# Two of four weight products in float16 pairs instead of float32r pairs, in a windowed-attention, SoLU-MoE and rational-MoE kernel

## The chip, the cores and the metric

The kernel runs on one core of a Trainium2 chip. The metric is the time of one execution on the device in microseconds, lower is better; before the change the median of three runs is 745.09 us (744.92 to 745.19).

## The reference

Attention with a causal window of 128 keys and a linear bias per head (4 batches, 8 heads, 576 positions, 64 wide) gives 2304 tokens of 512 numbers. Two feed-forward blocks follow. All is wanted in about float32 precision.

```python
scores = scale * q @ k.T + bias ; masked to 0 <= rel < 128 ; softmax ; @ v     # 2304 x 512
# first MoE, d_ff = 1024
h = x @ w_in
solu = h * softmax(h)
ln = (solu - mu) / np.sqrt(var + 1e-06) * g_ln
x = ln @ w_out
# second MoE, d_ff = 2048
h = x @ w_in
P = a[0] + a[1] * h + a[2] * h2 + a[3] * h3
Q = 1.0 + np.abs(b[0]) * np.abs(h) + np.abs(b[1]) * h2
out = (P / (Q + 1e-06)) @ w_out
```

## The kernel before, in words

Weights and inputs come as float64 where the reference gives them so; `decode` (lines 489 to 503) turns a raw piece of 128 x 512 into float32 with one ScalarE and two VectorE operations. Each of the four weight products then works on **pairs**: an operand is split into an upper part and the rest, both float32r, and three products (upper x upper, rest x upper, upper x rest) are summed in PSUM. So each product costs three TensorE passes.

The work runs in tiles of 128 tokens (18 of them). `scores` and `attend` do the attention of a tile, from tile 5 on in 16-bit parts whose transposes go by DMA (line 700). `moe_in` (780) is the first product of the first MoE: 24 matmuls of 512 columns a tile, at line 788. `moe_tr` (835) transposes its result into `lh`, `ll` at lines 845 and 846. `moe_out` (850) does two tiles at a time, 96 matmuls of 256 columns at line 863, with stationary `woh`, `wol` (w_out times the gains g_ln, split by `split_w`, 533), copies the sums into `ys` and stores them to `yT` in DRAM. The second MoE runs over groups of 512 tokens (four, and one of 256) and 16 steps `f` of 128 hidden units. `ff_in` (933) makes h in one PSUM bank with 12 matmuls at line 942, then eleven elementwise operations (lines 962 to 980) on ScalarE and VectorE, and the split into `gh`, `gl` (helpers `copy`, line 468 to 470, and `less`, line 479 and 480). `ff_out` (986) takes these as stationary operands of 12 matmuls of 512 columns at line 1003. Its weights come through `early_w2` (887), which decodes 28 pieces during the first stage and parks them in DRAM, and `split_w2` (901), which reloads and splits them; `load_y` (917) reloads and splits the tokens.

The order of all this is not written by hand. Each operation is put on a list with an engine (or several possible), a modelled duration and a due time `pri`; `Plan.order` (158) lays them out by a list schedule when the program is built, and the engines then execute that fixed order. The table `PR` holds the due times and offsets by stage and engine, `SLOTS` the number of buffers of each kind. Where TensorE would have nothing in the first 50 us of the plan, a filler matmul on zeros is put there (line 1073, bfloat16, 256 columns). SBUF has two regions a side: `left1` and `right1` for the first stage, `left2` and `right2` for the second MoE; a later region opens when the earlier one is wholly free.

Of the kernel before, what the change touches and what calls it, by code (L numbers as in the profile page):

```python
# [7 lines left out]
F32 = mybir.dt.float32  # L8
F32R = mybir.dt.float32r
# [14 lines left out]
    "bias": -3.593, "biash": -2.341, "load": 3.531, "load0": 5.238, "hold": 2, "merge": 8, "loadv0": 4.2,  # L24
    "loadv": 4.079, "v": 1.842, "s": 1.742, "pv": 0.742, "win": -1.048, "wout": 0.37, "wstep": 0.368,
    "tr": -0.218, "mo": 2.066, "e0": 3.565, "e1": 12.092, "npre": 28, "plain": 5, "ln": 'dve',
    "alt.dve": 1500.0, "alt.act": 393.9, "alt.pool": -274.9, "ahead": 5.989, "warm": 50000.0,
    "cold": 6800.0, "pein": 1, "peout": 0, "last": 0.16, "scores.dve": -0.358, "scores.pool": 0.961,
    "scores.pe": -0.3, "moe_in.dve": 0.79, "attend.act": -0.139, "moe_out.pool": 0.119,
    "scores.act": 0.342, "moe_in.act": 2.074, "attend.dve": 0.102, "moe_tr.pe": -0.442,  # L30
    "moe_out.dve": -0.69, "moe_out.act": 0.25, "split_v.dve": -0.139, "moe_out.pe": 0.224,
    "weights.dve": 0.16, "weights.act": -0.169, "weights.pool": -0.155,
# [289 lines left out]
def t_pe(n, cols, wide=True):  # L322

    return n * (cols * 0.4167 + ((17.0 if cols > 256 else 13.3) if wide else 4.0))
# [20 lines left out]
def kernel(  # L345
# [119 lines left out]
    def copy(out, i, n, r, w, pri, psum=False, first="act", on=("act", "dve", "pool")):  # L465

        alts = {
            "act": (t_act(n, psum), lambda: nc.scalar.activation(out=out(), in_=i(), func=ACTF.Copy), False),  # L468
            "dve": (t_dve(n, not psum), lambda: nc.vector.tensor_copy(out(), i()), not psum),
            "pool": (t_pool(n, False), lambda: nc.gpsimd.tensor_scalar(  # L470
                out(), i(), 1.0, 0.0, ALU.mult, ALU.add), True),
        }
# [59 lines left out]

# [582 lines left out]
```

## Time and profile before

| | |
|---|---|
| median of 3 runs | 745.09 us |
| span of the profiled execution | 744.7 us |
| TensorE busy / VectorE / ScalarE / GpSimd | 736.3 / 585.1 / 479.3 / 318.8 us |
| TensorE weight loads busy | 631.6 us |
| matmuls of line 863 / 942 / 1003 / 788 | 864 / 960 / 864 / 432 |

The median lies 0.4 us above the profiled span. In the profile PE is TensorE's matmuls, PEld its weight loads, DVE VectorE, ACT ScalarE, POOL GpSimd, SP the queue that issues DMAs. A matmul's recorded duration (371 ns on average at line 942) is its passage through a pipeline; the pace of a run of matmuls is read from the start-to-start distance, that is from the length of a run in the chain divided by its count.

### The profile page before, as it was taken

The page shows a single profiled execution, that of the slowest core. Times are in us where ns is not written, and L with a number is a line of the kernel's source. Part 1 is how long each engine was busy: PE and PEld are TensorE (multiplying, and loading weights), DVE is VectorE, ACT ScalarE, POOL GpSimd, SP SyncE. Part 2 cuts the span into 40 slices and gives each one's busy share as a digit, 9 for nine tenths or more (in the row PEclk, how much of TensorE's full clock was granted, in tenths as well). Part 3 has the DMA queues.
Part 4 walks back from the last instruction along what each step waited for, and adds up shares of the span by engine and source line. Part 5 has one row for each costly group of instructions (what it writes and reads, how often), then busy time and mean ns, then how long its engine had stood idle before and what let it go on. Part 6 is the DMA issues. An engine that isn't in the chain of part 4 may idle for free.

```text
span 744.7 us, 14059 instructions
## 1 busy us (share of the span) xinstructions
PE 736.3 (99%) x5184; PEld 631.6 (85%) x5184; DVE 585.1 (79%) x1259; ACT 479.3 (64%) x950; POOL 318.8 (43%) x319
## 2 busy tenths in 40 slices
PE   8999999999999999999999999999999999999997
PEld 7889989898898999899788888888888888888896
DVE  4999788887888754456989897779977788877984
ACT  6887665755656555365997776557755666566783
POOL 1524444445544734065895633334233443332421
PEclk9999999999999999999999999999999999999999
DMA  8933899999999835063651210000100001000010
GB/s 317 302 132 81 191 266 256 249 279 206 263 233 200 163 79 93 17 212 106 191 155 57 73 62 1 0 1 22 57 1 1 0 1 58 0 1 0 1 58 29
DMA packets 107349, 82.19 MB, mean 110 GB/s; under 512 B 57616, under 2 KB 89360, under 8 KB 107280
## 3 DMA queue, kind: packets, MB, share of 16 engines
q1 hardware_dynamic: 107280, 81.29, 41.3%
q8 instruction: 41, 0.67, 0.4%
q14 instruction: 28, 0.23, 0.1%
HBM read 51.39 MB, written 16.78 MB: 92 GB/s over the span
## 4 chain that ended last, share of the span: by engine, by line
PE 95%; DVE 2%; ACT 1%; DMA 1%; SPq 0%; issue 0%; POOL 0%; POOLq 0%; DVEq 0%
PE bk L942 26%; PE bk L1003 14%; PE h L788 14%; PE bk L863 13%; PE h L1003 11%; PE bk L639 4%; PE bk L768 4%; PE bk L616 3%; PE bk L743 2%; PE bk L1073 2%; PE bk L685 1%; DMA dx<-w2i 1%; DVE bk L965 0%; ACT s L669 0%; DVE bk L976 0%; DVE tcc L980 0%
## 5 line engine op out<-in xcount | busy, mean ns | idle before, releaser
L942 PE MATMUL bk<-yh,wb 128*128 128x512 f32 (+1 forms) x540 | 133.3, 371 | 0.2 <-DVE tcc L974 0.2
L480 POOL TENSOR_TENSOR gl<-tcc,gh 128x512 fp32r<-128x512 f32 x63 | 82.0, 1301 | 85.5 <-PE bk L1003 54.9
L942 PEld LDWEIGHTS bk<-yh,wb 128*128 128x128 f32 x540 | 97.2, 188 | 21.4 <-DVE tcc L974 0.4
L962 ACT ACTIVATE bk<-bk,bcoef 128x512 f32<-128x512 f32 (+1 forms) x80 | 49.6, 620 | 91.7 <-PE bk L942 91.6
L942 PE MATMUL bk<-yh,wa 128*128 128x512 f32 (+1 forms) x420 | 101.9, 371 | 1.1 <-DVE tcc L974 0.9
L942 PEld LDWEIGHTS bk<-yh,wa 128*128 128x128 f32 x420 | 75.0, 188 | 17.5 <-DVE tcc L974 1.7
L965 DVE SCALAR_TENSOR_TENSOR bk<-tb,nb,bk 128x512 f32<-128x512 f32 (+1 forms) x80 | 56.0, 700 | 42.7 <-ACT tb L964 42.6
L1003 PE MATMUL bk<-wo,gh 128*128 128x512 f32 x288 | 88.5, 394 | 0.0
L863 PE MATMUL bk<-lh,woh 128*128 128x256 f32 x288 | 84.1, 292 | 0.0
L863 PE MATMUL bk<-ll,woh 128*128 128x256 f32 x288 | 81.5, 283 | 0.0
L863 PE MATMUL bk<-lh,wol 128*128 128x256 f32 x288 | 81.4, 283 | 0.0
L669 ACT ACTIVATE s<-s,nm 128x256 f32<-128x256 f32 (+1 forms) x144 | 63.6, 489 | 19.9 <-DVE nm L662 19.7
L1003 PE MATMUL h<-wo,gh 128*128 128x512 f32 x240 | 74.9, 393 | 0.9 <-POOL gh L470 0.9
L470 POOL TENSOR_SCALAR gh<-tcc 128x512 fp32r<-128x512 f32 (+1 forms) x42 | 26.1, 622 | 94.9 <-DVE tcc L980 75.9
L480 POOL TENSOR_TENSOR pl<-s,ph 128x512 f16<-128x512 f32 (+1 forms) x51 | 61.4, 1215 | 9.0 <-ACT ph L468 6.2
L1003 PEld LDWEIGHTS bk<-wo,gh 128*128 128x128 f32 x288 | 53.4, 188 | 11.3
L976 DVE SCALAR_TENSOR_TENSOR bk<-bk,qc,tb 128x512 f32<-128x512 f32 (+1 forms) x80 | 56.3, 704 | 7.2 <-ACT tb L969 5.3
L662 DVE CUSTOM_DVE_ANT_0 s<-bk,bias 128x256 f32<-128x256 f32 (+1 forms) x144 | 50.9, 404 | 11.9 <-PE bk L639 10.4
L970 ACT ACTIVATE tcc<-bk,acoef 128x512 f32<-128x512 f32 (+1 forms) x80 | 59.3, 741 | 0.2 <-POOL gh L480 0.2
L967 ACT ACTIVATE tb<-bk,qc 128x512 f32<-128x512 f32 (+1 forms) x80 | 51.9, 648 | 11.3 <-DVE bk L965 10.9
L974 DVE SCALAR_TENSOR_TENSOR tcc<-tcc,acoef,bk 128x512 f32<-128x512 f32 (+1 forms) x80 | 55.5, 693 | 2.3
L980 DVE SCALAR_TENSOR_TENSOR tcc<-tcc,acoef,bk 128x512 f32<-128x512 f32 (+1 forms) x80 | 55.4, 693 | 2.2
(174 smaller groups left out, 1816.8 us busy)
## 6 DMA issues: line engine op xcount, KB each, us to landing
rw<-in_moe_w_in_dram SPq DMA_DIRECT2D x18, 512.0 KB, 4.9
rw<-in_moe_w_out_dram SPq DMA_DIRECT2D x16, 512.0 KB, 4.6
kn<-in_k_dram SPq DMA_DIRECT2D x18, 256.0 KB, 5.1
qn<-in_q_dram SPq DMA_DIRECT2D x18, 256.0 KB, 3.9
vv<-in_v_dram SPq DMA_DIRECT2D x18, 256.0 KB, 4.4
yT<-ys SPq DMA_DIRECT2D x18, 256.0 KB, 3.2
yr<-yT SPq DMA_DIRECT2D x16, 256.0 KB, 3.4
w2i<-dc SPq DMA_DIRECT2D x15, 256.0 KB, 3.4
```

The source lines that it names most:

```text
L480: "pool": (t_pool(n), lambda: nc.gpsimd.tensor_tensor(out(), a(), b(), op), True),
L669: nc.scalar.activation(out=s[:, jj, 0:W], in_=s[:, jj, 0:W], func=ACTF.Exp, scale=-1.0, bias=nm[:, h:h + 1], accum_out=sm[:, h:h + 1] if p ...
L788: nc.tensor.matmul(h[:, cols], a[:, kk], w[:, kk, cols], start=(i == 0 and kk == 0), stop=(i == 2 and kk == KD - 1))
L863: nc.tensor.matmul(y[:, r], w[:, f, cols], x[:, f % 4], start=(f == 0 and n == 0), stop=(f == KF - 1 and n == 2))
L942: nc.tensor.matmul(h(), w[:, a, kk], y[:, b, kk, 0:n], start=(i == 0 and kk == 0), stop=(i == 2 and kk == KD - 1))
L965: o("dve", t_dve(n) + 60, lambda: stt(out=A(), in0=R(), scalar=nb1, in1=A(), op0=ALU.mult, op1=ALU.subtract), [bR], [bA])
L967: o("act", t_act(n, True, ptrs=1), lambda: act(out=R(), in_=A(), func=ACTF.Ln, scale=-1.0, bias=qc), [bA], [bR])
L970: o("act", t_act(n, True, 2), lambda: act(out=C(), in_=h(), func=ACTF.Identity, scale=acoef[:, 3:4], bias=acoef[:, 2:3]), [hb, "coef"], [bC])
L974: o("dve", t_dve(n) + 60, lambda: stt(out=C(), in0=C(), scalar=acoef[:, 1:2], in1=h(), op0=ALU.add, op1=ALU.mult), [hb], [bC])
L976: o("dve", t_dve(n) + 60, lambda: stt(out=A(), in0=A(), scalar=qc, in1=R(), op0=ALU.subtract, op1=ALU.mult), [bR], [bA])
L980: o("dve", t_dve(n) + 60, lambda: stt(out=C(), in0=C(), scalar=acoef[:, 0:1], in1=A(), op0=ALU.add, op1=ALU.mult), [bA], [bC])
L1003: nc.tensor.matmul(acc[g][s][2](), a(slice(s * P, (s + 1) * P)), w[:, c], start=(f == 0 and i == 0), stop=(f == KF2 - 1 and i == 2))
```

## The change

`moe_out` and `ff_in` get float16 pairs where they had float32r pairs; `moe_in` and `ff_out` stay float32r. Since float16 has a narrow range, the weights are scaled by powers of two found on the chip. `squares` sums the squares of each of the 8 pieces of w_out (times g_ln) and of the 16 pieces of the second w_in on ScalarE. `scale_to_range` takes the largest sum, spreads it over the partitions by one TensorE product with ones, and makes a power of two and its inverse with some ten tiny VectorE operations. `scaled_gains` then splits all 8 pieces of w_out, which wait decoded in a float32 buffer `wof`; `split_w2` splits each piece of w_in by ScalarE or GpSimd and VectorE. The powers are taken back in factors that were there before (`hc` in place of the coefficients), in the copy to `ys` and in the copy of the outputs. The normalised tokens carry a factor 2^10.

The numbers of buffers and the due times are dealt anew, and the early pieces of the second MoE's w_in come sooner than those of w_out (16 and 12 of the 28, before 15 and 13).

```diff
 PR = {
-    "bias": -3.593, ... "loadv": 4.079, "v": 1.842, "s": 1.742, "pv": 0.742, "win": -1.048, "wout": 0.37, "wstep": 0.368,
-    "tr": -0.218, "mo": 2.066, "e0": 3.565, "e1": 12.092, "npre": 28, "plain": 5, "ln": 'dve',
-    ... "ahead": 5.989, ...
+    "bias": -1.592, ... "loadv0": 5.697, "loadv": 5.377, "v": 1.039, "s": 1.964, "pv": 0.916, "win": -1.733,
+    "wout": 0.079, "wstep": 0.041, "tr": -5.062, "mo": 2.534, "e0": 3.645, "e1": 12.42, "npre": 28,
+    ... "ahead": 1.425, ... "weights.dve": 2.246, "weights.act": -2.496, "weights.pool": -0.392,
 SLOTS
-        "e": 1, "u": 2, "lh": 2, "ll": 3, "rw": 2, "ys": 3, "dc": 3, "st": 6,
+        "e": 1, "u": 2, "lh": 2, "ll": 3, "rw": 2, "ys": 4, "dc": 3, "st": 5,
-        "qn": 2, "kn": 5, "vv": 3, "v2": 4, "s": 5, "ph": 1, "pl": 2, "pth": 3, "ptl": 3,
-        "xr": 3, "xh": 3, "xl": 4, "nm": 3, "sm": 3,
+        "qn": 2, "kn": 5, "vv": 3, "v2": 2, "s": 5, "ph": 1, "pl": 3, "pth": 3, "ptl": 2, "xr": 5,
+        "xh": 5, "xl": 6, "nm": 6, "sm": 3, "tn": 1,
-        "wa": 7, "woa": 1, "gh": 3, "gl": 2, "yh0": 1, "yr": 5, "wr": 1, "dx": 3, "tb": 2,
-        "tcc": 3,
+        "wa": 7, "woa": 1, "gh": 4, "gl": 2, "yh0": 1, "yr": 4, "wr": 4, "dx": 4, "tb": 3, "tcc": 8,
-        "wb": 9, "wo": 15, "yh1": 1, "ob": 3,
+        "wb": 9, "wo": 15, "yh1": 1, "ob": 2,
...
-    woh = w1.tile([P, KF, DM], F32R, name="woh")
-    wol = w1.tile([P, KF, DM], F32R, name="wol")
+    wof = w1.tile([P, KF, DM], F32, name="wof")
+    woh = w1.tile([P, KF, DM], F16, name="woh")
+    wol = w1.tile([P, KF, DM], F16, name="wol")
...
+    def squares(x, xa, at, key, pri, by=None):
+        plan.op("act", t_act(512, ptrs=1 if by is None else 2), lambda: nc.scalar.activation(
+            out=junk, in_=xa(), func=ACTF.Square, scale=1.0 if by is None else by(), accum_out=sums[:, at:at + 1]),
+            r=[x] + ([] if by is None else ["gsb"]), w=[key], pri=pri)
+
+    def scale_to_range(name, lo, hi, keys, pri):
...
+        tiny(lambda: V.tensor_reduce(out=top(), in_=sums[:, lo:hi], axis=AX.X, op=ALU.max), keys)
+        plan.op("dve", 200, lambda: V.tensor_scalar(d.t, ident, top(), None, ALU.mult), r=[m], w=[d], pri=pri)
+        plan.op("pe", 235.0, lambda: nc.tensor.matmul(b.t, ones, d.t, start=True, stop=True), r=[d], w=[b], pri=pri)
...
+    def scaled_gains(pri):
+        scale_to_range("o", 0, KF, [("sums", f) for f in range(KF)], pri)
...
+        for f in range(KF):
...
+            split_scaled(x, lambda f=f: wof[:, f], lambda f=f: woh[:, f], lambda f=f: wol[:, f],
+                         ("woh", f), ("wol", f), gain, "gs", pri)
...
-            part = (lambda: woh[:, f], lambda: wol[:, f], ("woh", f), ("wol", f))
-            gain = lambda: gsb[:, f:f + 1]
...
-                split_scaled(x, *part, gain, pri)
+            squares(x, xa, f, ("sums", f), pri, by=lambda: gsb[:, f:f + 1])
...
-            lT[pr] = [(Buf("lh", [P, 4, 2 * P], F32R), Buf("ll", [P, 4, 2 * P], F32R)) for _ in range(2)]
+            lT[pr] = [(Buf("lh", [P, 4, 2 * P], F16), Buf("ll", [P, 4, 2 * P], F16)) for _ in range(2)]
...
-            copy(lambda ys=ys: ys.t, lambda y=y: y.t, 512, [y], [ys], pri, psum=True)
+            copy(lambda ys=ys: ys.t, lambda y=y: y.t, 512, [y], [ys], pri, psum=True, by=2.0 ** -20)
...
+        if kind == "i":
+            squares(x, lambda: flat(x.t), KF + f, ("sums", KF + f), pri)
...
-        w = Buf(group, [P, 2] + shape2[kind], F32R)
+        w = Buf(group, [P, 2] + shape2[kind], F16 if kind == "i" else F32R)
...
-        split(x, lambda: x.t, lambda: w[:, 0], lambda: w[:, 1], (w, 0), (w, 1), 512, pri)
+        if kind == "i":
+            split_scaled(x, lambda: x.t, lambda: w[:, 0], lambda: w[:, 1], (w, 0), (w, 1),
+                         lambda: power["i"][:, 0:1], ("power", "i"), pri)
+        else:
+            split(x, lambda: x.t, lambda: w[:, 0], lambda: w[:, 1], (w, 0), (w, 1), 512, pri)
...
-        y = Buf(f"yh{g % 2}", [P, 2, KD, 512], F32R)
+        y = Buf(f"yh{g % 2}", [P, 2, KD, 512], F16)
...
-        o("act", t_act(n, True, 1), lambda: act(out=A(), in_=h(), func=ACTF.Abs, scale=bcoef[:, 0:1]),
-          [hb, "coef"], [bA])
+        o("act", t_act(n, True, 1), lambda: act(out=A(), in_=h(), func=ACTF.Abs, scale=hc[:, 4:5]),
+          [hb, "hc"], [bA])
...
         copy(lambda ob=ob: ob.t, src[2], 512, [src[1]], [ob], pri - 4.0, psum=True,
-                     first="act" if s % 2 != last else "dve")
+                     first="act" if s % 2 != last else "dve", by=lambda: hc[:, 2:3])
...
-    pieces = sorted([(f - 2.0, "i", f) for f in range(KF2)] + [(f, "o", f) for f in range(KF2)])
+    pieces = sorted([(f - 4.0, "i", f) for f in range(KF2)] + [(f, "o", f) for f in range(KF2)])
...
+    scaled_coefs(PR["e0"] + PR["e1"] + 0.3)
```

## Rows read from the trace of the kernel before

**Rows 1.** The page: busy time of each engine, and TensorE's granted clock in 40 slices.
```profile
PE 736.3 (99%) x5184; PEld 631.6 (85%) x5184; DVE 585.1 (79%) x1259; ACT 479.3 (64%) x950; POOL 318.8 (43%) x319
...
PEclk9999999999999999999999999999999999999999
```

**Rows 2.** Waits of engine PE: us in total, times, longest us.
```profile
PE bk L1073 <- DVE still L440: 1.8, 1, 1.8
PE bk L942 <- DVE tcc L974: 1.0, 3, 0.7
PE h L1003 <- POOL gh L470: 0.9, 1, 0.9
```

**Rows 3.** Stretches: length; PE, PEld, DVE, ACT, POOL busy us; PEclk; DMA share; GB/s.
```profile
20.00:50.00 30.00, 30.00 (x277) 26.54 (x276) 28.05 (x78) 26.61 (x73) 14.16 (x13) 1.00 0.75 252
50.00:100.00 50.00, 50.00 (x378) 44.76 (x378) 43.14 (x126) 35.67 (x80) 19.01 (x18) 1.00 0.59 146
...
150.00:200.00 50.00, 50.00 (x534) 45.19 (x531) 39.75 (x122) 30.43 (x64) 23.68 (x25) 1.00 1.03 245
...
300.00:350.00 50.00, 49.72 (x389) 45.06 (x388) 26.36 (x50) 24.20 (x46) 19.84 (x17) 1.00 0.35 111
350.00:400.00 50.00, 49.31 (x214) 39.70 (x213) 44.74 (x61) 43.00 (x74) 41.91 (x37) 1.00 0.49 153
400.00:420.00 20.00, 20.00 (x88) 16.17 (x87) 18.74 (x30) 13.13 (x21) 12.57 (x13) 1.00 0.15 53
420.00:440.00 20.00, 20.00 (x89) 16.39 (x88) 18.48 (x25) 16.27 (x28) 9.96 (x9) 1.00 0.24 75
...
550.00:600.00 50.00, 50.00 (x217) 40.46 (x217) 39.46 (x55) 29.15 (x49) 19.26 (x21) 1.00 0.00 0
```

**Rows 4.** Chain that ended last, in time: start us, us, what, matmuls in a row.
```profile
17.31 1.09 PE bk L1073 x10
...
36.47 1.73 PE bk L743 x16
...
114.03 1.24 PE bk L768 x40
...
332.82 11.51 PE bk L863 x96
```

**Rows 5.** Groups, shapes apart: count, busy us, mean ns, idle before: splits and sums.
```profile
L480 POOL TENSOR_TENSOR wb<-dx,wb 128x512 fp32r<-128x512 f32 x8 | 10.4, 1298 | 2.8 <-ACT wb L468 2.8
L480 POOL TENSOR_TENSOR wa<-dx,wa 128x512 fp32r<-128x512 f32 x7 | 9.8, 1416 | 0.9 <-ACT wa L468 0.7
L479 DVE TENSOR_TENSOR wo<-dx,wo 128x512 fp32r<-128x512 f32 x3 | 5.3, 1754 | 0.5 <-POOL wo L470 0.5
L519 DVE SCALAR_TENSOR_TENSOR wol<-dc,gsb,woh 128x512 fp32r<-128x512 f32 x6 | 5.0, 832 | 0.5 <-POOL woh L513 0.5
L815 ACT ACTIVATION_READ_ACCUMULATOR e<-u,st 128x1 f32 x18 | 3.4, 187 | 0.0
L511 ACT ACTIVATE woh<-dc,gsb 128x512 fp32r<-128x512 f32 x2 | 1.4, 716 | 0.9 <-DVE dc L501 0.9
```

**Rows 6.** Lines 519, 863 and 1073: count, min/median/max ns, first to last start in us.
```profile
L519 DVE SCALAR_TENSOR_TENSOR wol<-dc,gsb,woh x6: 745/750/1019, 39.4 to 80.2; 128x512 fp32r<-128x512 f32 x6
...
L863 PE MATMUL bk<-lh,woh x288: 277/283/385, 74.3 to 343.8; 128*128 128x256 f32 x144
...
L1073 PE MATMUL bk<-still x85: 272/273/422, 1.8 to 47.9; 128*128 128x256 bf16 x85
```

**Rows 7.** Groups, shapes apart: VectorE's slowest and quickest of six at lines 965 to 980.
```profile
L976 DVE SCALAR_TENSOR_TENSOR bk<-bk,qc,tb 128x512 f32<-128x512 f32 x64 | 48.5, 757 | 5.5 <-ACT tb L969 3.8
...
L973 DVE TENSOR_TENSOR tcc<-tcc,bk 128x512 f32<-128x512 f32 x64 | 43.8, 685 | 1.5 <-ACT tcc L970 1.4
```

**Rows 8.** Park of decoded weights in DRAM: w2i, count, ns, first to last start.
```profile
L895 SPq DMA_DIRECT2D w2i<-dc x15: 320/431/1400, 79.7 to 242.1; - x15
L907 SPq DMA_DIRECT2D dx<-w2i x15: 319/320/432, 319.0 to 386.2; - x15
```

More of the change, by code (lines that the diff above doesn't have):

```diff
@@ L23 @@
 PR = {
[L24 to L32 removed]
+    "bias": -1.592, "biash": -3.111, "load": 4.133, "load0": 6.849, "hold": 2, "merge": 8,
+    "loadv0": 5.697, "loadv": 5.377, "v": 1.039, "s": 1.964, "pv": 0.916, "win": -1.733,
+    "wout": 0.079, "wstep": 0.041, "tr": -5.062, "mo": 2.534, "e0": 3.645, "e1": 12.42, "npre": 28,
+    "plain": 5, "ln": "dve", "alt.dve": 5294.7, "alt.act": -1617.4, "alt.pool": -133.9,
+    "ahead": 1.425, "warm": 50000.0, "cold": 6800.0, "pein": 1, "last": -0.271, "scores.dve": -0.357,
+    "scores.pool": -4.451, "scores.pe": -0.644, "moe_in.dve": 0.677, "attend.act": -6.228,
+    "moe_out.pool": -1.535, "scores.act": 0.636, "moe_in.act": 2.094, "attend.dve": -0.224,
+    "moe_tr.pe": -5.891, "moe_out.dve": -0.048, "moe_out.act": -2.929, "split_v.dve": -1.37,
+    "moe_out.pe": -0.392, "weights.dve": 2.246, "weights.act": -2.496, "weights.pool": -0.392,
 }
@@ L319, in emit, with t_pe @@
             o.fn()
[L322 to L324 removed]
+def t_pe(n, cols, half=False):
+    return n * (cols * 0.4167 + (2.6 if half else 17.0 if cols > 256 else 13.3))
 def t_act(n, psum=False, ptrs=0):
@@ L438 @@
     qc = const.tile([P, 1], F32, name="qc")
+    ones = const.tile([P, P], F32, name="ones")
+    junk = const.tile([P, 512], BF16, name="junk")
+    sums = const.tile([P, KF + KF2], F32, name="sums")
+    gs = const.tile([P, KF], F32, name="gs")
+    hc = const.tile([P, 8], F32, name="hc")
+    power = {n: const.tile([P, 2], F32, name=f"power{n}") for n in "oi"}
+    nc.vector.memset(ones, 1.0)
     still = const.tile([P, 256], BF16, name="still")
@@ L463, with copy @@
     nc.vector.memset(v1r[:, :, :, D:D + 1], 1.0)
-    def copy(out, i, n, r, w, pri, psum=False, first="act", on=("act", "dve", "pool")):
+    def copy(out, i, n, r, w, pri, psum=False, first="act", on=("act", "dve", "pool"), by=1.0):
+        ptr = not isinstance(by, float)
+        scale = by if ptr else lambda: by
         alts = {
[L468 to L471, printed above, removed]
+            "act": (t_act(n, psum, int(ptr)), lambda: nc.scalar.activation(
+                out=out(), in_=i(), func=ACTF.Identity if ptr else ACTF.Copy, scale=scale()), False),
+            "dve": (t_dve(n, not psum) + 60 * ptr, lambda: nc.vector.tensor_copy(out(), i()) if by == 1.0 else
+                    nc.vector.tensor_scalar(out(), i(), scale(), None, ALU.mult), not psum),
+            "pool": (t_pool(n, False) + 60 * ptr, lambda: nc.gpsimd.tensor_scalar(
+                out(), i(), scale(), 0.0, ALU.mult, ALU.add), True),
         }
@@ new lines, in scaled_coefs @@
+    def scaled_coefs(pri):
+        scale_to_range("i", KF, KF + KF2, [("sums", KF + f) for f in range(KF2)], pri)
+        V = nc.vector
+        o, i = power["o"], power["i"]
+        at = lambda n: hc[:, n:n + 1]
+        r = [("power", "o"), ("power", "i"), "a", "b", "coef"]
+        for fn in (
+            lambda: V.tensor_scalar(at(0), o[:, 0:1], i[:, 0:1], 2.0 ** -10, ALU.mult, ALU.mult),
+            lambda: V.tensor_scalar(at(1), o[:, 1:2], i[:, 1:2], 2.0 ** 10, ALU.mult, ALU.mult),
+            lambda: V.tensor_scalar(at(2), at(1), at(1), None, ALU.mult),
+            lambda: V.tensor_scalar(at(3), acoef[:, 3:4], at(1), None, ALU.mult),
+            lambda: V.tensor_scalar(at(4), bcoef[:, 0:1], at(1), None, ALU.mult),
+            lambda: V.tensor_scalar(at(5), nb1, at(2), None, ALU.mult),
+            lambda: V.tensor_scalar(at(6), acoef[:, 1:2], at(0), None, ALU.mult),
+            lambda: V.tensor_scalar(at(7), acoef[:, 0:1], at(0), at(0), ALU.mult, ALU.mult),
+        ):
+            plan.op("dve", 110, fn, r=r, w=["hc"], pri=pri)
@@ L943, in mm @@
                                      start=(i == 0 and kk == 0), stop=(i == 2 and kk == KD - 1))
-            plan.op("pe", t_pe(KD, n), mm, r=[(w, a)] + [(y, b, kk) for kk in range(KD)],
+            plan.op("pe", t_pe(KD, n, True), mm, r=[(w, a)] + [(y, b, kk) for kk in range(KD)],
                     w=[hb], pri=pri)
```

74 lines of the change are left out of this document (47 added, 27 removed).

## The prediction

> **What bounds the kernel now.** I read the busy times first [rows 1]: TensorE is busy 736.3 of 744.7 us, VectorE 79%, ScalarE 64%, GpSimd 43%, and the granted clock is full (2.4 GHz) in every slice. A busy TensorE need not be a full one, so the second view is what TensorE waits for [rows 2]: 3.7 us in its three largest rows, the longest wait 1.8 us at the very start. The third is the pace, the test that counts. In the stretch from 550 to 600 us 217 matmuls begin, all of 512 columns (lines 942 and 1003), one every 50 / 217 = 230.4 ns [rows 3]; the 512 columns alone take 213.3 ns at 2.4 GHz. A run of 96 matmuls of line 863 takes 11.51 us, 119.9 ns each, against 106.7 ns for 256 columns [rows 4]. So the matmuls stand back to back, and the pace itself is longer than the columns: about 17 ns more per 512, 13 ns more per 256. Everything else hides behind TensorE. The next limit is VectorE: 39.46 of 50 us in that steady stretch, but 28.05 of 30 from 20 to 50 us, and 44.74 + 18.74 + 18.48 = 82.0 of 90 us from 350 to 440 us, where the first group of the second MoE also has weights to split [rows 3].
>
> **The change on TensorE.** No matmul of the two products is removed: 864 of 256 columns at line 863, and at line 942 768 of 512 columns (4 groups x 16 steps x 12) and 192 of 256. What changes is the pace. The trace has 16-bit matmuls: ten fillers of 256 bfloat16 columns take 1.09 us, 109 ns each, 2.3 ns above the columns; 40 matmuls of line 768 (64 or 65 columns, float16 weights, another weight tile nearly each time) take 1.24 us, 31 ns each, 4.2 ns above the 26.8 ns of their columns [rows 4]. So the extra time of a 16-bit matmul is bounded by 2.3 and 4.2 ns; I take 2.3, because the filler has the width of line 863, and keep 4.2 for the range.
>
> Line 863: 864 x (119.9 - 109.0) = 9.4 us less (by the other end 864 x 9.0 = 7.8). Line 942, 192 of the same width: 192 x 10.9 = 2.1 us less (1.7). For 512 columns no 16-bit row exists: 213.3 + 2.3 = 215.6 ns by the same extra, 2 x 109 = 218 ns if the extra grows with the columns, 230.4 if nothing is won. I take 215.6, since the extra per matmul is of one size at 64 and at 256 columns: 768 x (230.4 - 215.6) = 11.4 us less (9.5 at 218; the 230.4 is a rival below). Together 22.9 us less, 19.0 at the other ends.
>
> The Trainium skill ("TensorE: Matmul & The Clock Gate", section "Back-to-back issue gap") gives two figures for 512 columns: an isolated gap of N / 2.4 + 2.5 ns, with which the filler's 109 ns agrees, and a sustained 131 ns per matmul in a stream of weight loads and matmuls. The first leaves the sum as it is (215.8 ns, 0.2 us); the second is rival E. No row here has a matmul quicker than its columns at 2.4 GHz.
>
> Added on TensorE are two products of 128 float32 columns (one per power of two). The nearest rows are 16 matmuls of line 743, 64 float32 columns, in 1.73 us, 108 ns each [rows 4]; twice that, 0.22 us each, 0.4 us in all.
>
> **The other engines.** (1) Squares: 24 on ScalarE, each about 716 ns (a 128x512 pass with a pointer scale) + 187 ns for reading the accumulator [rows 5], 0.90 us, 21.7 us in all. Sixteen lie beside the early weights of the first stage, where ScalarE has 30.43 of 50 us [rows 3]: nothing. Eight (7.2 us) lie at the front, where from 20 to 50 us ScalarE is at 26.61 of 30. Before, the pieces of w_out were split one after the other (the row of VectorE's part has six of the eight, at 39.4 to 80.2 us) while the first product that reads them came at 74.3 us [rows 6]; now all 8 must be decoded and summed before one of them is split. From 50 to 100 us ScalarE has 14.3 us to spare [rows 3], so most of it fits ahead of the first use; and TensorE has fillers only until 47.9 us [rows 6]. Between 0 and 7.2 us; I take 1.0, near the cover. A gain is possible too, since the front is dealt anew (`xh` 5, `xl` 6): the 85 fillers at 109 ns are 9.3 us, of which those before the first inputs land can't be saved, so an estimated 5 us come back at most. I count none. (2) The chain of some ten tiny operations on VectorE per power is a few us long; the first is part of the wait just told, the second is due when the last piece of the second w_in is decoded. Those were parked from 79.7 to 242.1 us and read again only from 319.0 us on [rows 8], so some 70 us cover it: nothing. (3) The split of 16 pieces of w_in: GpSimd loses 8 subtractions of 1298 ns and 7 of 1416 ns (20.2 us), VectorE gains 16 of 832 ns, 13.3 us [rows 5]. Seven of them go into the first buffers `wa`, which fill from about 319 us, where VectorE has 26.36 of 50 us; nine fall into the stretch with 82.0 of 90 us [rows 3]. There 9 x 0.83 = 7.5 us make 89.5, and TensorE leaves 12 x 14.8 ns = 0.18 us less per step, some 3 us over the 16 steps of the group, so 87. But the three subtractions of 1754 ns that VectorE did for `wo` (5.3 us) [rows 5] can go to GpSimd, which has the 20.2 us free. So 84 of 87 us: tight, and covered; I take nothing, and price the other case as rival A. (4) Copies with a scale for `ys` and the outputs, float16 instead of float32r results: the same passes over the same columns, off TensorE's path, nothing. (5) DMA: the 28 early pieces are the same in number; from 150 to 200 us the DMA share reads 1.03 but 0.35 from 300 us on [rows 3], so there is room later. `ptl` and `v2` go from 3 and 4 buffers to 2 and 2: an attention tile must then hand its buffer over within one tile's time (18 tiles before 319 us, some 17 us each), and TensorE has other work queued: nothing, or a part of rival B.
>
> SP's queue carries the same transfers, with one early piece of w_in more and one of w_out less. The waits that the change adds stand on VectorE and ScalarE: behind the wait for all eight sums are queued the exponentials and score passes of the next tiles, for which TensorE waits; that is the 0 to 7.2 us above.
>
> **The sum.** 744.7 - 22.9 + 0.4 + 1.0 = 723.2 us of span; the median lay 0.4 us above the span, so 723.6 us.
>
> **The rivals.** *A, VectorE is late in the first group.* The new subtractions read two SBUF tiles on VectorE while GpSimd works on SBUF too. The `wo` rows show what that can cost: 1754 ns where the like of it at line 519 takes 745 alone [rows 5, 6]. If the nine take 1754 ns and GpSimd takes nothing back, VectorE has 82.0 + 15.8 = 97.8 us to do where TensorE leaves 87, and up to 10 us are lost: 727 to 733 us, say 730. For it: the stretch is the fullest of the trace. Against: GpSimd has less to do, so fewer collisions. The Trainium skill ("SBUF — State Buffer", "SBUF: two separate sides") has the port pair as an exclusive lock between VectorE with two SBUF inputs and GpSimd, which speaks against this part of the change; by it the 1754 ns are one wait for a GpSimd subtraction, as the rows' 745 + some 1000 ns suggest. *B, the front eats it.* All 7.2 us of squares and the wait for eight pieces are paid by TensorE in fillers and gaps, against what ScalarE has free: 723.6 + 4 to 10, say 729. *C, the 512 columns don't get quicker* (float32r's extra is not what costs there): 723.6 + 11.4 = 735. Against it are both 16-bit rows. *D, slower than before.* One mechanism: the power of two of w_out comes late. The buffers `lh` (2), `ll` (3) and `u` (2) hold two pairs of tiles at most, so once tiles 0 to 3 have passed `moe_in`, TensorE has attention alone until line 863 can begin, and VectorE feeds that. It began at 74.3 us [rows 6]; it decides when the first start slips by the saving, past 74.3 + 22 = 96 us with nothing to fill: then 745 to 755, say 750. For it: the sum over all eight is a new barrier; against: all eight pieces were split by 81 us before, at an even pace that the new due times pull forward. *E, TensorE falls below VectorE.* Were 16-bit matmuls of 512 columns so quick that a step of the second MoE took TensorE under 4.4 us, VectorE's six operations a step (685 to 757 ns each [rows 7], some 4.4 us) would bound it: 64 steps save 5.53 - 4.4 = 1.13 us each, 72 us where the sum has 11.4, about 663 us. No row has such a pace. The 131 ns of the Trainium skill's section named above would bring it about (12 x 131 + 12 x 230.4 ns = 4.3 us a step).
>
> **How the numbers follow.** Forecast 0.75, with its own range 718 to 727 (the gain and the loss at the front, the two ends of the pace); A 0.09, B 0.08, C 0.03, D 0.04, E 0.01. The range reaches from 718.5 to 732: it leaves out C, D, E and the worse parts of A and B, some 0.14 with the forecast's own tails. A measurement here can tell about 0.2% (1.5 us) from no change. Faster are the forecast, A, B, C and E, together 0.96, of which 0.02 go to the same (C with B, or a mild D): faster 0.94, same 0.02, slower 0.04.
>
> **What would show it.** Runs of line 863 at 109 ns a matmul and a steady stretch at (230.4 + 215.6) / 2 = 223 ns instead of 230.4; TensorE's waits still in single us; the first start of line 863 no later than some 85 us; VectorE from 350 to 440 us above 90% without TensorE waiting at line 942 or 1003. It is wrong if matmuls of line 942 keep 230 ns, if TensorE's idle time grows by more than 5 us, or if fillers and gaps ahead of 100 us grow by more than a few us.

## The result and the profile after

| | before | after |
|---|---|---|
| median of the runs | 745.14 us (744.92 to 745.4) | 727.5 us (725.57 to 728.51) |
| ratio, 95% interval | | 0.9759 (0.9744 to 0.9773) |
| span of the profiled execution | 744.7 us | 723.8 us (its own time 725.57 us) |
| TensorE busy / idle | 736.3 / 8.4 us | 715.4 / 8.4 us |
| VectorE, ScalarE, GpSimd | 79, 64, 43% | 81, 69, 42% |

The kernel is 17.6 us faster, 2.4%. The forecast was 723.6 us, the range 718.5 to 732.0.

The page of the changed kernel, its busy times and the granted clock:

```profile
PE 715.4 (99%) x5187; PEld 516.8 (71%) x5187; DVE 583.2 (81%) x1294; ACT 496.0 (69%) x1005; POOL 302.8 (42%) x309
...
PEclk9999999999999999999999999999999999999999
```

Beside [rows 1] the number of matmuls is the same but for three (one filler less, four records of the products with ones), and TensorE's idle time (span less busy) is 8.4 us in both kernels. So all of the gain is in busy time: in the pace. What TensorE waits for, in the changed kernel (us in total, times, longest us):

```profile
PE bk L1147 <- DVE still L445: 1.9, 1, 1.9
PE bk L1014 <- DVE ll L912: 1.2, 1, 1.2
PE bk L682 <- DVE u L892: 0.6, 1, 0.6
```

These are of the size of [rows 2]; the first is the start again. Lines have moved: 863 is now 929 (`moe_out`), 942 is 1014 (`ff_in`), 1003 is 1075 (`ff_out`), 1073 is 1147 (fillers), 519 is 526 (splits). Stretches of the changed kernel, to be laid beside [rows 3] (length; PE, PEld, DVE, ACT, POOL busy us; PEclk; DMA share; GB/s):

```profile
20.00:50.00 30.00, 29.86 (x276) 26.25 (x277) 26.95 (x87) 27.24 (x76) 9.21 (x9) 1.00 0.78 253
50.00:100.00 50.00, 49.92 (x397) 43.26 (x394) 43.63 (x129) 40.61 (x97) 20.88 (x20) 1.00 0.59 149
...
350.00:400.00 50.00, 50.00 (x223) 29.71 (x221) 48.91 (x68) 42.60 (x73) 35.72 (x30) 1.00 0.38 117
400.00:420.00 20.00, 20.00 (x90) 11.75 (x90) 18.27 (x27) 14.85 (x26) 15.22 (x15) 1.00 0.19 53
420.00:440.00 20.00, 20.00 (x90) 11.78 (x89) 17.74 (x26) 13.51 (x23) 6.67 (x7) 1.00 0.14 53
```

From 350 to 440 us TensorE is busy in all 90.00 us, and VectorE in 48.91 + 18.27 + 17.74 = 84.9. And the chain that ended last, in order of time (start us, us, what, matmuls in a row): 96 matmuls of `moe_out`, then blocks of the second MoE at two places:

```profile
327.41 10.48 PE bk L929 x96
...
461.47 0.88 PE bk L1014 x4
...
477.61 0.88 PE bk L1014 x4
...
558.58 0.88 PE bk L1014 x4
559.46 0.47 PE h L1075 x2
559.92 0.47 PE bk L1075 x2
560.39 0.88 PE bk L1014 x4
...
564.02 0.88 PE bk L1014 x4
```

The same in the kernel before:

```profile
461.59 0.92 PE bk L942 x4
...
478.15 0.92 PE bk L942 x4
...
548.13 0.93 PE bk L942 x4
...
553.71 0.93 PE bk L942 x4
```

`moe_out` takes 10.48 us / 96 = 109.2 ns a matmul, 119.9 before [rows 4]. In the second MoE a block of four matmuls of `ff_in` and four of `ff_out` goes round in (564.02 - 558.58) / 3 = 1.81 us, before in (553.71 - 548.13) / 3 = 1.86 us. At the other place, nine rounds long, it is (477.61 - 461.47) / 9 = 1.79 us, before (478.15 - 461.59) / 9 = 1.84. So neither kernel has one pace throughout, but the gain is 47 ns a block at both places, 12 ns for each 512-column float16 matmul, where the forecast had 14.8.

The size over the whole execution comes from the records of the two traces, with overlaps counted once: TensorE is busy with `moe_out` for 104.6 us before and 95.1 after, and with `ff_in` and `ff_out` together for 400.4 and 390.3. These sums, 9.5 and 10.1 us less, are used below; that of the second MoE lies between 390.3 and 390.6 us in the traces of after, e0, e1b, e3b and e9.

### The profile page after: what moved, and what is told of

It is laid out like the page before. It is cut to its first block, busy times and chain, and to the rows that moved or that the text cites. A ratio compares the mean times of both kernels' runs of the same rounds, so it can differ in the third digit from the quotient of the medians.

```text
span 723.8 us, 14095 instructions
## 1 busy us (share of the span) xinstructions
PE 715.4 (99%) x5187; PEld 516.8 (71%) x5187; DVE 583.2 (81%) x1294; ACT 496.0 (69%) x1005; POOL 302.8 (42%) x309
## 4 chain that ended last, share of the span: by engine, by line
PE 93%; ACT 3%; DVE 2%; DMA 1%; issue 1%; SPq 0%; POOL 0%; POOLq 0%; DVEq 0%; ACTq 0%
PE bk L1014 26%; PE bk L1075 15%; PE h L854 13%; PE h L1075 12%; PE bk L929 12%; PE bk L834 4%; PE bk L705 4%; PE bk L682 3%; PE bk L809 1%; PE bk L1147 1%; ACT s L735 1%; DVE s L728 1%; DMA yr<-yT 1%; ACT wof L506 1%; PE bk L751 0%
## 5 line engine op out<-in xcount | busy, mean ns | idle before, releaser
L1014 PE MATMUL bk<-yh,wb 128*128 128x512 f16 (+1 forms) x540 | 128.5, 360 | 0.0
L1034 ACT ACTIVATE bk<-bk,hc 128x512 f32<-128x512 f32 (+1 forms) x80 | 49.5, 619 | 97.4 <-PE bk L1014 97.2
L1014 PE MATMUL bk<-yh,wa 128*128 128x512 f16 (+1 forms) x420 | 96.8, 360 | 1.4 <-DVE ll L912 1.2
L1037 DVE SCALAR_TENSOR_TENSOR bk<-tb,hc,bk 128x512 f32<-128x512 f32 (+1 forms) x80 | 56.0, 700 | 43.1 <-ACT tb L1036 41.2
L929 PE MATMUL bk<-lh,woh 128*128 128x256 f16 x288 | 78.6, 273 | 0.0
L929 PE MATMUL bk<-lh,wol 128*128 128x256 f16 x288 | 78.5, 273 | 0.0
L929 PE MATMUL bk<-ll,woh 128*128 128x256 f16 x288 | 78.5, 273 | 0.0
L929 PEld LDWEIGHTS <-woh 128*128 128x128 f16 x576 | 56.3, 98 | 9.5 <-issue 2.9
L1042 ACT ACTIVATE tcc<-bk,acoef,hc 128x512 f32<-128x512 f32 (+1 forms) x80 | 59.3, 741 | 0.0
L1046 DVE SCALAR_TENSOR_TENSOR tcc<-tcc,hc,bk 128x512 f32<-128x512 f32 (+1 forms) x80 | 55.4, 693 | 2.3
```

What stands on the lines that cost most here:

```text
L929: nc.tensor.matmul(y[:, r], w[:, f, cols], x[:, f % 4], start=(f == 0 and n == 0), stop=(f == KF - 1 and n == 2))
L1014: nc.tensor.matmul(h(), w[:, a, kk], y[:, b, kk, 0:n], start=(i == 0 and kk == 0), stop=(i == 2 and kk == KD - 1))
L1037: o("dve", t_dve(n) + 60, lambda: stt(out=A(), in0=R(), scalar=hc[:, 5:6], in1=A(), op0=ALU.mult, op1=ALU.subtract), [bR], [bA])
L1042: o("act", t_act(n, True, 2), lambda: act(out=C(), in_=h(), func=ACTF.Identity, scale=hc[:, 3:4], bias=acoef[:, 2:3]), [hb, "hc"], [bC])
L1046: o("dve", t_dve(n) + 60, lambda: stt(out=C(), in0=C(), scalar=hc[:, 6:7], in1=h(), op0=ALU.add, op1=ALU.mult), [hb], [bC])
```

## The experiments

Each was timed beside the kernel before on the same chip, whose median was 745.5 us throughout. "After" below is 727.2 to 727.5 us. All edits are to the changed kernel.

| kernel | median (range), us | ratio, 95% interval | against after |
|---|---|---|---|
| e0_after | 727.16 (725.13 to 727.86) | 0.9749 (0.9736 to 0.9763) | 0 |
| e2_in2_f32r | 740.51 (739.65 to 741.64) | 0.9933 (0.9921 to 0.9945) | +13.3 |
| e1_out_f32r | 750.61 (749.94 to 755.82) | 1.0081 (1.0058 to 1.0104) | +23.4 |
| e1b_half_f32r | 730.79 (728.93 to 730.97) | 0.9793 (0.978 to 0.9807) | +3.6 |
| e3_given | 730.83 (730.17 to 732.15) | 0.9805 (0.9793 to 0.9818) | +3.7 |
| e3b_given_same_order | 725.17 (725.09 to 725.55) | 0.9727 (0.9713 to 0.974) | -2.0 |
| e5_by_twelve | 726.15 (725.3 to 726.75) | 0.9738 (0.9725 to 0.9751) | -1.0 |
| e6_out2_f16 | 712.75 (712.26 to 713.14) | 0.9559 (0.9546 to 0.9572) | -14.4 |
| e7_all_f16 | 716.13 (716.0 to 718.47) | 0.9613 (0.9599 to 0.9628) | -11.0 |
| e4_more_dve | 737.8 (736.88 to 738.38) | 0.9895 (0.9881 to 0.991) | +10.6 |
| e8_old_times | 746.27 (744.28 to 748.95) | 1.001 (0.9997 to 1.0022) | +19.1 |
| e9_old_buffers | 727.52 (726.74 to 728.21) | 0.9758 (0.9746 to 0.9771) | +0.4 |

**The change again (e0).** No edit.

> The changed kernel once more, beside the three kernels below. Theory P (the gain is TensorE's pace: 13.5 us at line 1014, 9.3 us at line 929, less some 2 us for switching between float16 and float32r matmuls 9 ns at a time): 727.5 us again, 2.4% under the kernel before. Its executions spread over 3 us (725.6 to 728.5) where those of before spread over 0.5. Theory S: one marginal wait, at the change of buffers near 316 us (TensorE idle 1.3 us there in the first profile), is longer in other executions; then a second profile shows 2 to 4 us there. Rival: the spread lies elsewhere or everywhere, and the stretch around 316 us reads 1.3 us again.

This second profile has a span of 725.6 us and TensorE busy in 716.8: of the 1.8 us between the two profiles only some 0.4 is idle time. The second falls behind by 0.7 us in the first 20 us and by the rest in steps of a few tenths before 325 us, and the stretch around 316 us takes only some 0.4 of it. So no single wait decides between a quick and a slow execution, and theory S falls. The kernel before scatters by as much (744.72 to 746.65), so 1 us is what a comparison of medians is worth here.

**The second w_in in float32r again (e2).**

```diff
-        w = Buf(group, [P, 2] + shape2[kind], F16 if kind == "i" else F32R)
+        w = Buf(group, [P, 2] + shape2[kind], F32R)
...
-        y = Buf(f"yh{g % 2}", [P, 2, KD, 512], F16)
+        y = Buf(f"yh{g % 2}", [P, 2, KD, 512], F32R)
...
-        ... "gh": 4, ... "wr": 4, "dx": 4, "tb": 3, "tcc": 8,
+        ... "gh": 3, ... "wr": 1, "dx": 3, "tb": 2, "tcc": 3,
```

> The second MoE's input product back in float32r pairs (weights and tokens), with the second region's buffers as before since the wider tiles need the room; powers and factors stay. Theory P: 768 x (230.4 - 215.6 ns) + 192 x (119 - 109 ns) = 13.3 us more, less 2 us because no matmul changes its type any more: 11.3 us more, 738.8 us (737 to 741). Rival: a float16 matmul among float32r ones gains little, 730 to 734 us; or the larger buffers were half the gain, above 743 us.

The cost is 13.3 us, in the range that the pace was given. TensorE is busy with `ff_in` and `ff_out` for 402.4 us, 12.0 more than in after. Its idle time is 737.5 - 728.1 = 9.4 us, 1.0 more; a wait of 1.3 us for `tcc`, of which there are now fewer, is new. The planned cost of `ff_in` goes back with the type, so the second MoE was laid out anew; that shows in no more than this 1 us. The pace carries this part.

**The first w_out in float32r again, whole (e1) and half (e1b).** In e1 each piece is split as soon as its squares are taken, so the order in which the planner lays out the front changes with it. In e1b only pieces 4 to 7 of w_out and of the left side are float32r, the planned costs are untouched, and the order of all instructions stays.

```diff
 e1
-    woh = w1.tile([P, KF, DM], F16, name="woh")
+    woh = w1.tile([P, KF, DM], F32R, name="woh")
...
-            lT[pr] = [(Buf("lh", [P, 4, 2 * P], F16), Buf("ll", [P, 4, 2 * P], F16)) for _ in range(2)]
+            lT[pr] = [(Buf("lh", [P, 4, 2 * P], F32R), Buf("ll", [P, 4, 2 * P], F32R)) for _ in range(2)]
 e1b
+    woh0 = w1.tile([P, 4, DM], F16, name="woh0")
+    woh1 = w1.tile([P, 4, DM], F32R, name="woh1")
...
+            lT[pr] = [(Buf("lh", [P, 4, 2 * P], t), Buf("ll", [P, 4, 2 * P], t)) for t in (F16, F32R)]
```

> The first MoE's output product back in float32r pairs, each piece of w_out split as soon as it is decoded; the sums of squares and the powers are still made, the second MoE is as changed. Theory P: 864 matmuls x (119.9 - 109.2 ns) = 9.3 us more than the changed kernel, 736.8 us (735 to 739). Rival B (the front pays for the wait on all eight pieces): that wait is gone too, so less is lost, 729 to 734 us.

> The changed kernel in its own order, instruction for instruction; only pieces 4 to 7 of w_out and the tokens' half that meets them are stored as float32r, so that 432 of the 864 matmuls of line 929 run in float32r (all of them would not fit beside the second region's buffers). Theory P (pace): 432 x (119.9 - 109.2 ns) = 4.6 us more, and some 0.3 us for switches of type: 732 us against 727.2 (731 to 733.5). Rival O (the due times and the order made the gain, not the type): 726 to 728.5 us. The whole product set back with a new order cost 23 us; by theory P 9.3 us of these are pace and the rest is the order of the front.

e1 lost 23.4 us, far more than either theory allowed. Its waits of TensorE say where (us, times, longest):

```profile
PE bk L676 <- DVE xr L806: 3.7, 1, 3.7
...
PE bk L676 <- POOL u L888: 1.9, 1, 1.9
```

TensorE's idle time is 748.6 - 730.7 = 17.9 us instead of 8.4, 7.7 of it from 50 to 100 us. So e1 measures a new order of the front, and what the type costs can't be read from it. e1b does that: 432 matmuls of float32r at 10.7 ns more each are 4.6 us (busy with `moe_out` 100.1 us, 5.0 more), measured +3.6 with a scatter of about 1. That is just under the 731 to 733.5 us of the pace theory and 2 us above the range of the rival, in which the type does nothing. The pace theory holds for `moe_out` too.

**The powers of two given, not found (e3, e3b).** In e3 the squares and the search are left out of the plan, and two constants (2^8 and 2^13) stand in their place; in e3b they stay in the plan, and its order, but issue nothing.

```diff
 both
+        nc.vector.memset(power[n][:, 0:1], 2.0 ** e)
...
 e3
-            squares(x, xa, f, ("sums", f), pri, by=lambda: gsb[:, f:f + 1])
 e3b
-        plan.op("act", t_act(512, ptrs=1 if by is None else 2), lambda: nc.scalar.activation(
-            out=junk, in_=xa(), func=ACTF.Square, scale=1.0 if by is None else by(), accum_out=sums[:, at:at + 1]),
+        plan.op("act", t_act(512, ptrs=1 if by is None else 2), lambda: None,
```

> The two powers of two are written as constants: no squares, no sums, no largest value, and a piece of w_out is split as soon as it is decoded (left out: finding the powers on chip). Theory P: the finding is hidden beside TensorE's other work, 727 us, within 1.5 us of the changed kernel. Rival B (the front pays): 720 to 724 us.

> The changed kernel in its own order, without the instructions that find the powers of two (no squares, sums, largest value, bit operations; the powers are constants); w_out's pieces are still split at the same place of the order. Theory P: 726.5 us, within 1.0 us of the changed kernel's 727.2: the finding is hidden. Rival B (the front pays for it): 720 to 724.5 us. The 730.8 us of the kernel that split each piece at once would then be its new order alone.

e3 left work out and came 3.7 us slower; both theories fell there. The planner had dealt a new front again (67 fillers instead of 84, waits of 1.6 and 1.4 us that after doesn't have), and TensorE's idle time is 11.7 us for 8.4. With the order frozen, finding the powers costs 2.0 us. That fits neither range: theory P allowed 1.0 us, rival B wanted 2.7 or more. It lies between the 1.4 that the sum had (0.4 + 1.0) and the 7.2 at which the front would have paid all eight squares. The pieces of it in after (groups, shapes apart: count, busy us, mean ns, idle before):

```profile
L542 ACT ACTIVATE junk<-wof,gsb 128x512 bf16<-128x512 f32 x8 | 5.8, 722 | 0.1
L542 ACT ACTIVATION_READ_ACCUMULATOR junk<-wof,gsb 128x1 f32 x8 | 1.6, 196 | 0.0
L560 PE MATMUL bk<-tn,ones 128*128 128x128 f32 x4 | 1.0, 320 | 0.0
```

ScalarE's 7.4 us are near the 7.2 of the forecast; the product with ones is four records of 320 ns (they overlap), where the sum had two of 220.

**Blocks of twelve (e5).** `ff_in` and `ff_out` are each issued as one run of twelve matmuls instead of three of four dealt alternately.

```diff
-            plan.op("pe", t_pe(KD, n, True), mm, r=[(w, a)] + [(y, b, kk) for kk in range(KD)],
-                    w=[hb], pri=pri)
+            passes.append(mm)
+        plan.op("pe", t_pe(3 * KD, n, True), lambda: [f() for f in passes],
+                r=[(w, 0), (w, 1)] + [(y, b, kk) for b in range(2) for kk in range(KD)], w=[hb], pri=pri)
```

> In the second MoE the twelve float16 matmuls of a step stand together, and the twelve float32r ones, where the changed kernel deals them in fours: two switches of type a step instead of six. Theory W (a pair of switches costs 9 ns): 240 pairs become 80, 1.4 us less, 725.7 us (724.5 to 727). Rival: with twelve at a time TensorE has to wait for the second split part (gl), which came during the fours before: 729 to 736 us.

The chain of e5 at the same two places:

```profile
463.47 2.60 PE bk L1015 x12
...
468.88 2.60 PE bk L1015 x12
...
557.91 2.60 PE bk L1015 x12
...
563.31 2.60 PE bk L1015 x12
```

Twelve and twelve take 563.31 - 557.91 = 5.40 us, where three blocks of after take 5.44; at the other place they take 5.41, where three of after take 5.38. So the price of a change of type can't be read from one stretch. Over the whole trace TensorE is busy with the two lines for 389.5 us, 0.8 less than in after. The 240 pairs of changes (192 blocks of 512 columns and 48 of 256) have become 80, so by this a pair costs 0.8 / 160 = 5 ns, 1.2 us for all that after has. The time, 1.0 us less and in the range that was expected, agrees, but alone it would be no more than the scatter.

**The second w_out in float16 too (e6), and all four products (e7).** Both take the same kind of scale out again in factors that were there (e7 with one tiny VectorE operation more a tile). The planned costs follow the types, so the order is dealt anew in both.

```diff
 e6
-            out=xa(), in_=hi().bitcast(F32), func=ACTF.Prelu, scale=2.0 ** -112, alpha=-2.0 ** 32),
+            out=xa(), in_=hi().bitcast(F32), func=ACTF.Prelu, scale=2.0 ** (up // 8 - 112), alpha=-2.0 ** 32),
...
-            bh, bl = (Buf(nm, [P, 512], F32R) for nm in ("gh", "gl"))
+            bh, bl = (Buf(nm, [P, 512], F16) for nm in ("gh", "gl"))
 e7, besides
-    wih = w1.tile([P, KD, FF], F32R, name="wih")
+    wih = w1.tile([P, KD, FF], F16, name="wih")
...
-        xh = Buf("xh", [P, KD, P], F32R)
+        xh = Buf("xh", [P, KD, P], F16)
```

> The second MoE's output product in float16 pairs too (its weights decoded 2^8 larger, the polynomial's coefficients scaled so that its result is 2^10 large, both taken back in the last copy). Theory P: 864 matmuls x 14.8 ns = 12.8 us less and no switches of type any more, 2 us: 712.4 us (710.5 to 714.5). Rival A (VectorE bounds the first group: in the changed kernel it is busy 84.9 of 90 us from 350 to 440 us, and TensorE would leave it 3 us less there): 714.5 to 718 us, with TensorE waiting between 330 and 430 us.

> All four weight products in float16 pairs: as the kernel with the second MoE's output in float16 (712.75 us), and the first MoE's input product as well (its weights decoded 2^8 larger, the tokens scaled by 2^8 in the copy, 2^16 taken back in the exponential, one tiny operation more a tile). Theory P: 432 matmuls x 14.8 ns = 6.4 us less, 706.4 us (705 to 709). Rival: in the first stage VectorE and the DMA queues, not the pace, set the end once TensorE is quicker: 709.5 to 713 us.

e6 came out at 712.75 us where 712.4 was expected: 14.4 us less than after, and faster than both kernels. Its chain has no change of type left:

```profile
558.57 0.86 PE bk L1016 x4
...
562.03 0.86 PE bk L1016 x4
```

(562.03 - 558.57) / 2 = 1.73 us a block; over five blocks 1.726, which is 215.8 ns a matmul, the 215.6 of the forecast. This pace, unlike float32r's, is the same in all of the second MoE: 165 of its 166 uninterrupted blocks take 1.72 to 1.73 us. TensorE is busy with the two products for 374.4 us, 15.9 less than in after. And the stretches (columns as above):

```profile
350.00:400.00 50.00, 50.00 (x234) 22.65 (x232) 48.09 (x72) 44.57 (x78) 34.23 (x32) 1.00 0.39 122
400.00:420.00 20.00, 20.00 (x94) 9.03 (x93) 17.91 (x27) 15.27 (x27) 14.00 (x14) 1.00 0.19 54
420.00:440.00 20.00, 20.00 (x94) 9.10 (x93) 18.32 (x27) 15.93 (x27) 6.01 (x7) 1.00 0.14 52
```

Even with a TensorE that is another 5% quicker in this group, VectorE is not late. e7 got the pace of the fourth product too (where matmuls of `moe_in` follow one another they start 216 ns apart in the median, 230 in after), but came 3.4 us slower than e6, beyond both ranges that were expected. Its span has 17.5 us of idle TensorE where e6 has 8.3; 6.0 of this lie between 70 and 100 us, and 2.6 more than in e6 between 320 and 340. The largest wait of e7, and three stretches of it (columns as above):

```profile
PE bk L684 <- DVE st L892: 4.6, 1, 4.6
```

```profile
80.00:85.00 5.00, 1.78 (x48) 1.53 (x46) 5.00 (x8) 2.63 (x7) 2.40 (x2) 1.00 0.70 157
85.00:90.00 5.00, 3.63 (x17) 2.80 (x18) 5.00 (x20) 3.44 (x8) 1.95 (x3) 0.52 0.29 54
90.00:95.00 5.00, 5.00 (x39) 4.50 (x38) 4.58 (x21) 4.10 (x11) 2.14 (x2) 0.80 0.82 95
```

VectorE is busy in all ten us from 80 to 90 while TensorE waits for it for 4.6 of them, and `moe_out` starts at 87.3 us (80.4 in after, 82.2 in e6). Whether all four products reach the expected 706 us or so with due times fitted to them was not tried.

**More work for VectorE in the first group (e4).** In that group alone VectorE copies each step's PSUM tile of `ff_in` to a spare buffer: 16 copies of 686 ns, 11.0 us.

```diff
+        if g == 0:
+            o("dve", t_dve(n), lambda: V.tensor_scalar(spare, h(), 1.0, None, ALU.mult), [hb], [])
```

> The changed kernel with one VectorE operation more in each of the first group's 16 steps (a pass over 128x512 in PSUM into a tile that nobody reads, about 0.68 us each, 11 us in all). In the changed kernel VectorE is busy 48.9 + 18.3 + 17.7 = 84.9 of 90 us from 350 to 440 us, and TensorE does not wait there. Theory E (the group is at VectorE's edge: 5 us free): some 5 us are lost, 732 us (730 to 735). Rival: the steps ahead and the buffers carry it into the next group, where VectorE is 80% busy: 727 to 728.7 us.

The 5 us that VectorE has free there (84.9 of 90) were expected to take up half of it. They took up next to nothing: the loss is 10.6 us, and 8.0 us of it are idle time of TensorE from 320 to 440 us. Two stretches of e4, and its largest wait:

```profile
400.00:420.00 20.00, 17.87 (x76) 9.48 (x75) 19.34 (x32) 12.44 (x21) 8.09 (x8) 1.00 0.00 0
420.00:440.00 20.00, 17.61 (x76) 9.82 (x75) 16.95 (x24) 16.38 (x29) 15.19 (x13) 1.00 0.23 69
```

```profile
PE bk L1015 <- DVE tcc L1049: 3.9, 3, 1.7
```

TensorE waits at `ff_in` for VectorE although VectorE itself has gaps (16.95 of 20). A reason could be that its passes and ScalarE's follow one another, so that a free us between them is of no use to another pass; that isn't shown. The planner saw the copies and dealt this group anew (no DMA from 400 to 420 us, where after has some), so how much of the 10.6 us is the order stays open. TensorE waiting for VectorE, rival A's mechanism, can be had here with 11 us more; after doesn't show it.

**The old due times (e8), the old numbers of buffers (e9).** Each alone, the types and the scales as in after.

```diff
 e8
-    "bias": -1.592, ... "wout": 0.079, "wstep": 0.041, "tr": -5.062, ... "weights.act": -2.496,
+    "bias": -3.593, ... "wout": 0.37, "wstep": 0.368, "tr": -0.218, ... "weights.act": -0.169,
 e9
-        "xh": 5, "xl": 6, "nm": 6, "sm": 3, "tn": 1,
+        "xr": 3, "xh": 3, "xl": 4, "nm": 3, "sm": 3, "tn": 1,
-        "wa": 7, "woa": 1, "gh": 4, "gl": 2, "yh0": 1, "yr": 4, "wr": 4, "dx": 4, "tb": 3, "tcc": 8,
+        "wa": 7, "woa": 1, "gh": 3, "gl": 2, "yh0": 1, "yr": 5, "wr": 1, "dx": 3, "tb": 2,
```

> The changed kernel with the due times and offsets of the kernel before, its own buffers kept. Theory O (each kernel's due times fit its own front; new orders of the front cost 4 us where the powers were given and some 13 us where the first MoE's output was set back): 732 us or more, the loss ahead of 100 us as idle time and fillers of TensorE. Theory P (the due times are worth little, the float16 pace is all): 727 to 730 us.

> The changed kernel with the numbers of buffers of the kernel before (one for the spread of the sums added), its due times kept. Theory O (what was dealt anew belongs together): 731 us or more. Theory P: 727 to 730 us, for TensorE hardly waited in the kernel before with these numbers.

The buffers are worth nothing that can be measured. Without the new due times the whole gain is gone: e8 stands at 746.27 us, level with the kernel before. That doesn't make the due times its source. The kernel before with new due times alone was not run, but its idle time (8.4 us) and fillers (85) are those of after (8.4 and 84), and the types set back one by one (e1b, e2) cost what their pace gives. Lines 526 and 929 in after (count, min/median/max ns, first to last start):

```profile
L526 DVE SCALAR_TENSOR_TENSOR wol<-wof,gs,woh x8: 733/740/1653, 74.6 to 81.4; 128x512 f16<-128x512 f32 x8
...
L929 PE MATMUL bk<-lh,woh x288: 269/273/283, 80.4 to 337.4; 128*128 128x256 f16 x144
```

and in e8, with its two largest waits of TensorE:

```profile
L526 DVE SCALAR_TENSOR_TENSOR wol<-wof,gs,woh x8: 737/1048/1651, 86.8 to 93.7; 128x512 f16<-128x512 f32 x8
...
L929 PE MATMUL bk<-lh,woh x288: 270/273/422, 98.2 to 349.4; 128*128 128x256 f16 x144
```

```profile
PE bk L682 <- DVE st L880: 3.5, 1, 3.5
PE bk L1014 <- POOL wa L524: 3.0, 1, 3.0
```

The eight pieces of w_out are split 12 us later, `moe_out` starts at 98.2 us, and TensorE runs out of other work: from 70 to 100 us it is idle for 5.6 us. In all its idle time is 743.3 - 721.8 = 21.5 us, 13.1 more than in after: 7.1 more from 70 to 130 us, 1.7 less from 130 to 320, 6.2 more from 320 to 380 (the weights of the second MoE come late too) and 1.7 more after 670. The other 6.4 us between the two profiles are busy time; the granted clock of 75 to 100 us reads 0.95, which can be no more than a part of it.

## Why the prediction was right

**The bound and the mechanism.** TensorE bounded the kernel by its pace, and the change bought pace: idle time 8.4 us in both, busy time 20.9 us less. Against the medians (17.6 us, 18.3 in e0) the traces give 9.5 us for `moe_out`, 10.1 for `ff_in` and `ff_out` together, and 2.0 back for the powers (e3b): 17.6. The rest of the 20.9 us lies in the two executions that were profiled, one above its kernel's median, the other below. e1b, e2 and e6 each move one product's type, and land within some 2 us of what its pace gives.

**`moe_out`, forecast 9.4 us.** 9.3 by the run of 96, 9.5 by the busy time: 109.2 ns where the filler's 109 was taken. Right, and so was the choice of that row for the price, the nearest in width.

**`ff_in`, forecast 11.4 us for the 512 columns and 2.1 for the 256.** These terms were mis-sized: 10.1 together. 47.5 ns a block (1.86 - 1.8125 us) times 192 is 9.1; for the 256 columns the chains have 0.938 us a block of four and two before and 0.917 after, times 48 is 1.0. The pace of pure float16 was right (215.8 ns in e6 for 215.6), and the 230.4 ns of before is a fair mean of the 1.86 and 1.84 us a block (232.5 and 230 ns a matmul). What the forecast put at nothing without a reason is that the two types stand side by side: it priced `ff_in` as if alone and left `ff_out` as it was. Of the 3.4 us that are missing, the changes of type explain some 1.2 (e5). The other 2 stay open: in e5 twelve of each still take 5.40 us, where e6's pace and before's at that place add up to 12 x (215.8 + 232.5) ns = 5.38, and 5.41 for 5.35 at the other. No row of before showed the two types side by side at this width, and the forecast gave that no bound. The Trainium skill ("TensorE: Matmul & The Clock Gate", section "Back-to-back issue gap") gives the two figures that were weighed: its isolated gap (N / 2.4 + 2.5 ns, 215.8 at 512 columns) is what e6 shows, and its sustained 131 ns, rival E, shows nowhere.

**The powers, forecast 0.4 + 1.0.** 2.0 by e3b, 0.6 more than the sum; the 0 to 7.2 us of the range held it, and a value near the cover was the better choice. The first start at 80.4 us stays under the 85 that the forecast named.

**VectorE in the first group, forecast 84 of 87 us, nothing lost.** 84.9 of 90 busy, and no wait of TensorE at `ff_in` in it (403 matmuls begin there, 391 before). GpSimd took all 15 subtractions of `wo` back, as was guessed, while the nine splits cost more than the 832 ns of the sum (after, groups by shape):

```profile
L526 DVE SCALAR_TENSOR_TENSOR wb<-dx,poweri,wb 128x512 f16<-128x512 f32 x9 | 10.7, 1185 | 0.0
...
L490 POOL TENSOR_TENSOR wo<-dx,wo 128x512 fp32r<-128x512 f32 x15 | 20.1, 1346 | 3.5 <-ACT wo L476 3.3
```

1185 ns lies between the two rows that bounded it [rows 5], and the trace shows why. One of the nine, with the GpSimd pass that was running when it began (start us, us):

```profile
350.94 1.31 POOL L490 TENSOR_TENSOR gl<-tcc,gh 128x512 fp32r<-128x512 f32 x1
351.23 1.57 DVE L526 SCALAR_TENSOR_TENSOR wb<-dx,poweri,wb 128x512 f16<-128x512 f32 x1
```

It ends at 352.80, 0.55 us after the other. Of the 24 passes of line 526 in after, 15 began while a GpSimd pass ran, among them all nine here, and each ended 0.54 to 0.55 us after that pass did; the nine others took 734 to 752 ns. The port lock of the Trainium skill ("SBUF — State Buffer", "SBUF: two separate sides"), by which VectorE with two SBUF inputs and GpSimd shut each other out for a whole instruction, agrees. So the case against rival A, fewer collisions, did not hold: all nine collided, for some 0.4 us each. TensorE did not wait all the same. That "84 of 87 us" would have held against more is not shown: e4, dealt anew, paid for nearly its whole addition.

**From span to median.** The 0.4 us that was added stood for two things. In every execution of either kernel the time is 1.8 us above its own span, so before's profiled execution (744.7 + 1.8) was 1.4 us above its median. The net was right, by luck: no row of before told the two apart.

**The rivals.** By the number alone A or B would do better: 727.5 us lies just above the 718 to 727 that the forecast gave itself, inside A's 727 to 733 and at B's 723.6 + 4. Only the wider range holds it. It is the waits and e3b that speak against both: TensorE doesn't wait from 350 to 440 us, in e6 not even with a quicker pace, and the powers cost 2.0 us, not the 4 to 10 of B. A and D can both be had here (e4, e8); after shows neither. D's point was that `moe_out` starts past 96 us, its price 745 to 755: e8 started it at 98.2 and took 746.3. The price came out by another sum than the one told, though, since 7.9 of the 13.1 us of added idle time lie past 320 us. What the forecast counted as hidden (the squares, the wait for eight pieces) is hidden under the new due times; it said that these pull the splits forward, gave the other case 0.04, and had no number for what they carry. e8 sets all of them back at once, so which of them matter stays open. C fell with 109.2 and 215.8 ns, E with both.

## What to carry to other kernels

Where TensorE is busy to the last us, price a type by what a matmul takes beyond its columns times the number of matmuls, from the nearest row of that type; then leave room for two types side by side if no row shows them so, and read a pace at more than one place (float32r blocks took 1.86 us at one and 1.84 at another). Where the order is planned from costs and due times, undoing one part measures a new order (e1, e3): keep the order and empty or halve the operations in it (e1b, e3b). A sum over all pieces ahead of the first use is a barrier whose cover is only as good as the due times (e8), and a few free us of the next engine are not a reserve until a run has shown it (e4).
